# Rounding the running expert maximum to f16 on GpSimd instead of ScalarE, in a fused attention and max-out feed-forward kernel

## The chip, the cores and the metric

The kernel runs on one core of a Trainium2 chip. The metric is device time in microseconds; three runs of the kernel before gave 973.61, 969.4 and 974.53 us, a median of 973.61. Five engines of the core work side by side, each through its own queue in program order: TensorE (PE; its weight loads are shown apart as PEld), VectorE (DVE), ScalarE (ACT), GpSimd (POOL) and SyncE (SP), which issues most transfers. An instruction that waits holds up everything behind it in its own queue.

## The reference

Causal attention with a cumulative bias, for 8 batches of 8 heads, 576 positions and head size 64, and behind it a feed-forward layer that takes the largest of three projections:

```
scores = scale * q @ k.T + min(-(cum[q] - cum[k]), 0)     # causal; cum = cumsum(max(s, 0))
attn   = exp(scores - max) / (sum + 1e-9)
x      = (attn @ v), heads side by side                    # 4608 tokens x 512
h      = max(max(x @ w1, x @ w2), x @ w3)                  # 4608 x 768
out    = h @ w_out                                         # 4608 x 512
```

The products are kept near f32 by splitting an operand into an f16 part and the f16 remainder of it: a product is then three matmuls (high by high, high by low, low by high). For `h`, the high part is called `hh` and the remainder `hl = h - hh`.

## The kernel before

**Attention** is cut into visits (a batch and a pair of heads) and these into 160 steps, each a block of 128 query positions. One step t goes through the engines like this: TensorE makes the scores in a PSUM bank `s` (two banks, so the scores of step t+2 need the bank that step t leaves); VectorE takes the row maximum `nm` (L447, function `highest`); ScalarE takes the exponential and its sum (L457, L461, `expo`); VectorE the reciprocal `ri` (L480); ScalarE writes the probabilities rounded to f16, `prh` and for the last block `tl` (L496); VectorE writes their remainder `prl` (L499), after which the bank is free; SyncE transposes both by DMA, and TensorE multiplies them with the values (`av`, L552). ScalarE and VectorE evict that as `x` and its remainder (L562, L563).

**Feed-forward work** fills TensorE's time between the attention matmuls. When the 256 or 320 tokens of a set are complete (16 sets: 8 batches, each in two parts), `add_set` queues 18 `h_group`s (6 blocks of 128 hidden features, `ft`, by 3 experts, `i`), each of 12 matmuls into a PSUM tile `pm` (L679), and 4 `o_group`s of 18 matmuls into `po` (L721). An eviction follows each `h_group`: for expert 0 ScalarE copies `pm` to the SBUF tile `m` (L693); for experts 1 and 2 VectorE takes the larger of `pm` and `m` into `m` (L696). After expert 2 the function `rest` splits `m`: ScalarE writes `hh` (L685), and GpSimd `hl` (L686). The `o_group`s need `hh` and `hl` of all six blocks, in the order of the blocks; `o` is evicted by ScalarE (L729) with a scale `os` from GpSimd (L714).

**The order** is that in which the program is written out; nothing is reordered afterwards. In step t the main loop (L877) writes: the reciprocal and `prh` of t; `nm` of t+1; `prl` of t and its transposes; then `drain()`, the evictions that are pending, and `flush()`, every `rest` that they have left; perhaps one feed-forward group; the scores of t+2; the exponentials of t+1; `drain()` and `flush()` again; what prepares later steps (on ScalarE L150, L154, L346 and others, on VectorE L159, L351, on GpSimd L137 to L168); more groups, as long as a running cost estimate allows; and the `av` matmuls of a visit. So a `rest` of the first `flush()` stands on ScalarE ahead of the exponentials of the next step, and on GpSimd among the casts and subtractions that prepare the heads of later visits.

Of the kernel before, what the change touches and what calls it, by code (L numbers as in the profile page):

```python
# [14 lines left out]
AF = mybir.ActivationFunctionType  # L15
# [6 lines left out]
def kernel(  # L22
# [9 lines left out]
    nc = tc.nc  # L32
# [149 lines left out]
    def load_w(i, dma=None):  # L182
# [14 lines left out]
        out=tri, in_=tri, pattern=[[-1, P]], compare_op=ALU.is_ge, fill=NEG, base=0, channel_multiplier=1  # L197
    )
    nc.gpsimd.memset(tri4, 0.0)
    for j in range(2):  # L200
        r = slice(j * D, (j + 1) * D)
        nc.gpsimd.affine_select(
            out=tri4[r], in_=tri4[r], pattern=[[-1, D]], compare_op=ALU.is_ge, fill=NEG, base=0, channel_multiplier=1
# [457 lines left out]
    def drain():  # L661
        while pending:
            pending.pop(0)()

    def add_set(b, ph):
        q0, nq = PH[ph]
        t0 = b * S + q0
        u = f"{b}_{ph}"
        xs = [(t[:, i, 0], t[:, i, 1]) for t in X.pop((b, ph)) for i in range(2)]
        st = {}  # L670

        def h_group(ft, i):
            pm = ps_m.tile([P, 512], F32, tag="m", name=f"pm{u}_{ft}_{i}")
            w = W[3 * ft + i]
            n = 0
            for kt in range(NKT):
                xh, xl = xs[kt]
                for wt, xt in ((0, xh), (0, xl), (1, xh)):
                    nc.tensor.matmul(  # L679
                        pm[:, :nq], lhsT=w[:, wt, kt, :], rhs=xt, start=(n == 0), stop=(n == 3 * NKT - 1)  # L680
                    )
                    n += 1

            def rest(m1):
                nc.scalar.activation(out=st["hh"][:, ft, :nq], in_=m1[:, :nq], func=AF.Copy)  # L685
                nc.gpsimd.tensor_tensor(  # L686
                    out=st["hl"][:, ft, :nq], in0=m1[:, :nq], in1=st["hh"][:, ft, :nq], op=ALU.subtract
                )

            def ev():  # L690
                if i == 0:
                    st["m1"] = moe.tile([P, 320], F32, tag="m1", name=f"m1{u}_{ft}", bufs=3)
                    nc.scalar.activation(out=st["m1"][:, :nq], in_=pm[:, :nq], func=AF.Copy, scale=HSC)  # L693
                else:
                    m1 = st["m1"]
                    nc.vector.scalar_tensor_tensor(  # L696
                        out=m1[:, :nq], in0=pm[:, :nq], scalar=HSC, in1=m1[:, :nq], op0=ALU.mult, op1=ALU.max
                    )
                if i == 2:
                    if not st.get("hh"):  # L700
                        st["hh"] = moe.tile([P, NFT, 320], F16, tag="hh", name=f"hh{u}")
                        st["hl"] = moe.tile([P, NFT, 320], F16, tag="hlo", name=f"hl{u}")
                    later.append(lambda m1=st["m1"]: rest(m1))

            pending.append(ev)
            if (ft, i) == (NFT - 1, 2):
                done.add((b, ph))

        def o_group(dt):
            drain()  # L710
            flush()
            if dt == 0:
                st["os"] = small.tile([P, 1], F32, tag="os", name=f"os{u}")
                nc.gpsimd.tensor_scalar(  # L714
                    out=st["os"], in0=OS[b, ph if b < NB else 1], scalar1=WS["kw"], scalar2=None, op0=ALU.mult
                )
            pm = ps_m.tile([P, 512], F32, tag="m", name=f"po{u}_{dt}")
            n = 0
            for ft in range(NFT):
                for wt, ht in ((0, "hh"), (0, "hl"), (1, "hh")):  # L720
                    nc.tensor.matmul(  # L721
                        pm[:, :nq], lhsT=W[18 + ft][:, wt, dt, :], rhs=st[ht][:, ft, :nq],
                        start=(n == 0), stop=(n == 3 * NFT - 1),
                    )
                    n += 1

            def ev():
                o_t = moe.tile([P, 320], F32, tag="m1", name=f"o{u}_{dt}", bufs=3)
                nc.scalar.activation(out=o_t[:, :nq], in_=pm[:, :nq], func=AF.Copy, scale=st["os"])  # L729
                nc.sync.dma_start(out=outT[dt * P:(dt + 1) * P, t0:t0 + nq], in_=o_t[:, :nq])  # L730

            pending.append(ev)

        for ft in range(NFT):
            for i in range(3):
                queue.append((lambda ft=ft, i=i: h_group(ft, i), (3 * ft + i,), 12 * nq * NSEC))
        for dt in range(NDT):
            queue.append((lambda dt=dt: o_group(dt), range(18, 24), 18 * nq * NSEC))
# [3 lines left out]
    def flush():  # L742
        while later:
            later.pop(0)()
# [224 lines left out]
```

## Time and profile before

| | before |
|---|---|
| median of three runs | 973.61 us (969.4 to 974.53) |
| the profiled execution: span from its first to its last instruction | 972.4 us; the profile gives no other total for it |
| PE / ACT / DVE / POOL busy | 847.3 / 599.1 / 589.2 / 285.2 us |
| `hh` on ScalarE (L685) | 96 times, 42.3 us busy; ScalarE idle in front of them 105.3 us |
| `hl` on GpSimd (L686) | 96 times, 73.9 us busy; GpSimd idle in front of them 459.8 us |

A profile line names the line of the kernel, the engine, the operation and its tiles (written <- read, shapes as partitions x elements), then times. In a timeline the first number is the start and the second the duration in us, and a bracket gives the engine's idle time in front of the instruction and what ended it. "x2" merges two instructions of one kind. An arrow "A <- B" in a list of waits reads: A waited for B. A PE matmul's end is modelled, so its busy time contains the pipeline's length; back to back, matmuls overlap.

### The profile page before, as it was taken

What the parts mean: (1) busy time and instruction counts of PE and PEld (TensorE: products, weight loads), DVE (VectorE), ACT (ScalarE), POOL (GpSimd) and SP (SyncE); (2) the same over time, 40 slices, a digit from 0 to 9 for tenths busy, and PEclk for the clock granted to TensorE, in tenths of its full rate; (3) what the DMA queues carried; (4) which work ended last, traced back from release to release, by engine and by line L of the source; (5) the groups of instructions that cost most, each with busy time, mean ns of one, the idle gap of its engine ahead of it and who ended that gap; (6) DMA issues with size and microseconds to landing.
All of it is one profiled execution on the core that took longest, in us unless ns stands there. A gap on an engine that the chain in (4) does not pass through costs nothing. (4 is left out here: it accounts for less than half of the span.)

```text
span 972.4 us, 19924 instructions
## 1 busy us (share of the span) xinstructions
PE 847.3 (87%) x7192; PEld 658.6 (68%) x7192; DVE 589.2 (61%) x1216; ACT 599.1 (62%) x1598; POOL 285.2 (29%) x455
## 2 busy tenths in 40 slices
PE   2547759997889967999999998999999999999998
PEld 2435547775557746876788777877787778777876
DVE  6898876656546665656666566665666666554111
ACT  4657566565547676676667676666676676765121
POOL 2001221212333432333333433444343433320101
PEclk9756979999889978999999999999999999999999
DMA  8952245477467777676868676875867776734000
GB/s 299 261 149 61 82 89 128 109 134 141 93 134 145 132 159 134 126 151 117 155 115 151 120 159 111 151 140 121 150 114 143 130 156 115 140 66 97 5 24 28
DMA packets 242035, 122.34 MB, mean 126 GB/s; under 512 B 217808, under 2 KB 226512, under 8 KB 241936
## 3 DMA queue, kind: packets, MB, share of 16 engines
q1 hardware_dynamic: 237904, 108.74, 56.8%
q10 hardware_dynamic: 4032, 12.32, 4.1%
q8 instruction: 57, 0.93, 0.4%
q14 instruction: 42, 0.34, 0.2%
HBM read 60.18 MB, written 9.44 MB: 72 GB/s over the span
## 5 line engine op out<-in xcount | busy, mean ns | idle before, releaser
L679 PE MATMUL pm<-x,w 128*128 128x256 f16 (+1 forms) x3456 | 461.0, 290 | 10.9 <-DVE x L563 5.6
L679 PEld LDWEIGHTS <-w 128*128 128x128 f16 x3456 | 335.0, 99 | 99.3 <-issue 11.5
L499 DVE SCALAR_TENSOR_TENSOR prl<-s,ri,prh 128x512 f16<-128x512 f32 (+3 forms) x288 | 153.0, 568 | 109.4 <-ACT prh L496 75.5
L686 POOL TENSOR_TENSOR hl<-m,hh 128x256 f16<-128x256 f32 (+1 forms) x96 | 73.9, 770 | 459.8 <-ACT hh L685 429.8
L496 ACT ACTIVATE prh<-s,ri 128x512 f16<-128x512 f32 (+3 forms) x288 | 141.6, 538 | 41.5 <-DVE ri L480 31.3
L457 ACT ACTIVATE s<-s,nm 128x512 f32<-128x512 f32 (+4 forms) x288 | 150.9, 524 | 9.7 <-DVE nm L447 5.5
L721 PE MATMUL po<-hh,w 128*128 128x256 f16 (+1 forms) x768 | 153.0, 290 | 3.1 <-ACT hh L685 3.0
L696 DVE SCALAR_TENSOR_TENSOR m<-pm,m 128x256 f32<-128x256 f32 (+1 forms) x192 | 87.2, 454 | 106.3 <-PE pm L679 91.7
L447 DVE TENSOR_REDUCE nm<-s 128x1 f32<-128x576 f32 (+4 forms) x160 | 127.7, 798 | 37.0 <-PE s L382 24.4
L721 PEld LDWEIGHTS <-w 128*128 128x128 f16 x1152 | 111.9, 99 | 33.7 <-issue 5.5
L721 PE MATMUL po<-hl,w 128*128 128x320 f16 (+1 forms) x384 | 111.2, 290 | 1.6 <-POOL hl L686 1.6
L685 ACT ACTIVATE hh<-m 128x256 f16<-128x256 f32 (+1 forms) x96 | 42.3, 440 | 105.3 <-DVE m L696 105.3
L562 ACT ACTIVATE x<-av 128x256 f16<-128x256 f32 (+1 forms) x64 | 26.3, 411 | 78.4 <-PE av L552 78.3
L693 ACT ACTIVATE m<-pm 128x256 f32<-128x256 f32 (+1 forms) x96 | 38.9, 405 | 52.6 <-PE pm L679 52.4
L168 POOL TENSOR_TENSOR l<-raw,h 64x576 fp32r<-64x576 f32 x48 | 67.9, 1414 | 2.3 <-ACT h L154 0.7
L376 PE MATMUL s<-h 128*128 128x128 f32 (+1 forms) x192 | 54.9, 368 | 15.1 <-DVE prl L499 11.8
L563 DVE SCALAR_TENSOR_TENSOR x<-av,x 128x256 f16<-128x256 f32 (+1 forms) x64 | 29.1, 454 | 64.1 <-ACT x L562 64.1
L137 POOL CAST l<-kb 64x576 fp32r<-64x576 f32 x48 | 31.9, 666 | 113.0 <-PE s L391 100.7
L552 PEld LDWEIGHTS <-vh 128*64 128x64 f16 x832 | 45.0, 114 | 22.3 <-issue 13.4
L552 PE MATMUL av<-ph,vh 128*64 128x320 f16 (+3 forms) x384 | 57.9, 293 | 2.3 <-DMA ph<-prh 2.3
L729 ACT ACTIVATE o<-po,os 128x256 f32<-128x256 f32 (+1 forms) x64 | 31.9, 498 | 45.1 <-PE po L721 28.6
L552 PE MATMUL av<-pl,vh 128*64 128x320 f16 (+3 forms) x384 | 57.1, 285 | 2.8 <-DMA pl<-prl 2.5
(138 smaller groups left out, 1108.8 us busy)
## 6 DMA issues: line engine op xcount, KB each, us to landing
raw<-in_qk_dram SPq DMA_DIRECT2D x96, 304.0 KB, 4.8
r<-in_w_dram ACTq DMA_DIRECT2D x20, 512.0 KB, 4.8
rv<-in_qkv_dram SPq DMA_DIRECT2D x32, 320.0 KB, 3.3
out_dram<-o SPq DMA_DIRECT2D x32, 160.0 KB, 2.2
out_dram<-o SPq DMA_DIRECT2D x32, 128.0 KB, 2.2
raw<-in_qkv_dram SPq DMA_DIRECT2D x8, 480.0 KB, 3.8
ph<-prh SPq DMA_TRANSPOSE x192, 3.3
pl<-prl SPq DMA_TRANSPOSE x192, 2.8
```

What stands on the lines that cost most here:

```text
L168: nc.gpsimd.tensor_tensor(out=l[far, QP:V0], in0=raw[far, QP:V0], in1=h[far, QP:V0].bitcast(F32), op=ALU.subtract)
L376: nc.tensor.matmul(ps[:, j, :nk], lhsT=w[:, qs], rhs=w[:, QP:QP + nk], start=(x == "h"), stop=False, skip_group_check=True,)
L447: nc.vector.tensor_reduce(out=nm, in_=sc, axis=AX.X, op=ALU.max, negate=True)
L457: nc.scalar.activation(out=sc, in_=sc, func=AF.Exp, bias=nm[:, j:j + 1], accum_out=sm[:, j:j + 1])
L496: nc.scalar.activation(out=hi, in_=src, func=AF.Copy, scale=sc)
L499: nc.vector.scalar_tensor_tensor(out=lo, in0=src, scalar=sc, in1=hi, op0=ALU.mult, op1=ALU.subtract)
L552: nc.tensor.matmul(av[j * D:(j + 1) * D, c0:nq], lhsT=lt, rhs=rt, start=(n < 2), stop=(n >= len(todo) - 2), skip_group_check=True,)
L679: nc.tensor.matmul(pm[:, :nq], lhsT=w[:, wt, kt, :], rhs=xt, start=(n == 0), stop=(n == 3 * NKT - 1))
L685: nc.scalar.activation(out=st["hh"][:, ft, :nq], in_=m1[:, :nq], func=AF.Copy)
L686: nc.gpsimd.tensor_tensor(out=st["hl"][:, ft, :nq], in0=m1[:, :nq], in1=st["hh"][:, ft, :nq], op=ALU.subtract)
L696: nc.vector.scalar_tensor_tensor(out=m1[:, :nq], in0=pm[:, :nq], scalar=HSC, in1=m1[:, :nq], op0=ALU.mult, op1=ALU.max)
L721: nc.tensor.matmul(pm[:, :nq], lhsT=W[18 + ft][:, wt, dt, :], rhs=st[ht][:, ft, :nq], start=(n == 0), stop=(n == 3 * NFT - 1),)
```

## The change

One line of `rest` changes: the f16 copy `hh` of the running maximum is made by GpSimd, directly in front of the subtraction that reads it.

```diff
             def rest(m1):
-                nc.scalar.activation(out=st["hh"][:, ft, :nq], in_=m1[:, :nq], func=AF.Copy)
+                nc.gpsimd.tensor_copy(out=st["hh"][:, ft, :nq], in_=m1[:, :nq])
                 nc.gpsimd.tensor_tensor(
                     out=st["hl"][:, ft, :nq], in0=m1[:, :nq], in1=st["hh"][:, ft, :nq], op=ALU.subtract
                 )
```

On ScalarE, at the second block (`m_1_1`) of one set in the long middle of the program: `prh` and `tl` are the probabilities of a step, `hh` the rounding, `s` and `se` the exponentials and sum of the next step.

```order
 L496 ACTIVATE prh_7202<-s_7071,ri_7200 128x512
 L496 ACTIVATE tl_7204<-s_7071,ri_7200 128x64
-L685 ACTIVATE hh_1_7135<-m_1_1_7166 128x320
 L457 ACTIVATE s_7154,sm_7240<-s_7154,nm_7155 128x128 x2
 L461 ACTIVATE se_7243<-sm_7240 128x2
```

The exponentials of the next step now follow the probabilities directly. Two blocks later in the same set, again on ScalarE:

```order
 L457 ACTIVATE s_7277,sm_7398<-s_7277,nm_7278 128x384 x2
 L461 ACTIVATE se_7401<-sm_7398 128x2
 L154 ACTIVATE h_1_7297<-raw_1_7168 128x576
 L496 ACTIVATE prh_7425<-s_7277,ri_7423 128x3x128 x2
-L685 ACTIVATE hh_1_7135<-m_1_3_7371 128x320
 L457 ACTIVATE s_7390,sm_7461<-s_7390,nm_7391 128x512 x2
 L461 ACTIVATE se_7464<-sm_7461 128x2
```

Here too the probabilities and the next exponentials become neighbours. The same stretch of the set on GpSimd, where `h` and `l` are the two parts of a head's queries and keys for a later visit:

```order
 L142 MEMSET l_1_7298 64x64
 L143 CAST l_1_7298<-qr_362 64x64
+L685 CAST hh_1_7135<-m_1_2_7245 128x320
 L686 TENSOR_TENSOR hl_1_7136<-m_1_2_7245,hh_1_7135 128x320
 L163 CAST l_1_7298<-h_1_7297 64x640
+L685 CAST hh_1_7135<-m_1_3_7371 128x320
 L686 TENSOR_TENSOR hl_1_7136<-m_1_3_7371,hh_1_7135 128x320
 L137 CAST l_0_7470<-kb_359 64x576
```

Each cast stands directly in front of its subtraction. The orders on TensorE and VectorE are the same as before.

## The prediction

> **What bounds the kernel now.** I read the page's busy times first, then the engines by stage, then who waits for whom in the long middle stage, and last the timeline around TensorE's waits. First the page's busy line, and the engines in the two stages that hold the change (busy time and instruction count of each engine, granted TensorE clock, DMA share, GB/s):
>
> ```profile
> PE 847.3 (87%) x7192; PEld 658.6 (68%) x7192; DVE 589.2 (61%) x1216; ACT 599.1 (62%) x1598; POOL 285.2 (29%) x455
> ...
> 92.00:391.00 299.00, 247.75 (x2042) 187.71 (x2040) 189.10 (x372) 187.39 (x482) 83.31 (x119) 0.91 0.60 122
> 391.00:893.00 502.00, 481.51 (x4241) 378.61 (x4239) 312.07 (x641) 341.99 (x932) 181.68 (x286) 1.00 0.70 131
> ```
>
> The rounding starts at 92 us, and after 893 attention is over, which leaves these two. From 391 to 893 us TensorE is busy 481.5 of 502 us at full clock: nothing there can be worth more than 20.5 us. From 92 to 391 us it idles 51 us, and the clock averages 0.91.
>
> So an average ("ACT 62%") tells nothing; the question is what ends TensorE's 20.5 idle us in the middle, and whether the rounding stands in that chain. Waits, 391 to 893 us (waiter, releaser: us in total, times, longest):
>
> ```profile
> PE s L376 <- DVE prl L499: 9.1, 14, 1.0
> PE s L391 <- DVE prl L499: 5.1, 5, 1.0
> PE pm L679 <- DVE x L563: 4.7, 4, 1.2
> ...
> ACT hh L685 <- DVE m L696: 50.5, 40, 2.2
> ```
>
> TensorE mostly waits for the score bank that VectorE's prl (L499) frees. And ScalarE stands still 50.5 us in front of the very instruction that is moved, with the next step's exponentials queued behind it. The L391 wait comes 5 times, so the stage has five like repeats of some 100 us. In each stands such a place, called A:
>
> ```profile
> 534.44 5.05 PE L679 MATMUL pm<-x,w 128*128 128x320 f16 x36
> ...
> 535.28 0.41 DVE L447 TENSOR_REDUCE nm<-s 128x2 f32<-128x256 f32 x1
> ...
> 536.53 0.32 ACT L496 ACTIVATE tl<-s,ri 128x64 f16<-128x64 f32 x1
> ...
> 537.74 1.08 DVE L696 SCALAR_TENSOR_TENSOR m<-pm,m 128x320 f32<-128x320 f32 x2
> 538.86 0.47 ACT L685 ACTIVATE hh<-m 128x320 f16<-128x320 f32 x1 [2.01 <-DVE m L696]
> ...
> 539.23 0.32 ACT L457 ACTIVATE s<-s,nm 128x128 f32<-128x128 f32 x1
> ...
> 540.31 0.42 ACT L693 ACTIVATE m<-pm 128x320 f32<-128x320 f32 x1
> 540.63 0.82 ACT L346 ACTIVATE vh<-rv,inv 128x640 f16<-128x640 f32 x1
> 541.35 0.62 ACT L496 ACTIVATE prh<-s,ri 128x128 f16<-128x128 f32 x2
> ...
> 542.75 0.59 PE L376 MATMUL s<-h 128*128 128x384 f32 x2 [1.04 <-DVE prl L499]
> ```
>
> Read from the bottom: TensorE idles 1.04 us, for a prl that waited for prh, which stood behind L346, L693 and the exponential, which stood behind the rounding, which waited 2.01 us for VectorE's maximum. The exponential's own input, nm, was ready at 535.69.
>
> **The change part by part.** *Removed from ScalarE*: 96 activations. *Added to GpSimd*: 96 casts. The activation, the subtraction behind it, and the nearest casts on GpSimd (count; busy us, mean ns; idle before):
>
> ```profile
> L685 ACT ACTIVATE hh<-m 128x256 f16<-128x256 f32 (+1 forms) x96 | 42.3, 440 | 105.3 <-DVE m L696 105.3
> ...
> L686 POOL TENSOR_TENSOR hl<-m,hh 128x320 f16<-128x320 f32 x48 | 40.3, 840 | 216.8 <-ACT hh L685 205.8 <-DMA raw<-in_qk_dram 7.4 <-PE s L382 3.6
> L138 POOL CAST l<-qr 64x512 fp32r<-64x512 f32 x48 | 29.5, 614 | 0.0
> L143 POOL CAST l<-qr 64x64 fp32r<-64x64 f32 x48 | 12.0, 251 | 0.0
> ```
>
> ScalarE loses 42.3 us of work. The two cast rows give (614 - 251)/448 = 0.81 ns an element over about 199 ns: 0.41 us for 256 columns, 0.46 for 320, on the mean what ScalarE took. Bounds: not under the 0.25 of the smallest cast, and not over the 0.84 of the two-input subtraction. I take 0.41 and 0.46, the same operation on the same engine, though no row has an f16 output; in all some 42 us more on GpSimd, which is busy 182 of 502 us in the middle.
>
> *The hand-over.* The subtraction now waits for its own engine. A dependent pair on GpSimd stands in the trace, and beside it the tightest place, where the output matmuls need the last hl:
>
> ```profile
> 126.46 0.21 POOL L631 TENSOR_SCALAR rtd<-rtd 128x1 f32<-128x1 f32 x1
> 126.76 0.27 POOL L635 TENSOR_SCALAR kw<-rtd,rtu 128x1 f32<-128x1 f32 x1
> ...
> 922.29 0.42 ACT L685 ACTIVATE hh<-m 128x256 f16<-128x256 f32 x1 [2.63 <-DVE m L696]
> 922.78 0.67 POOL L686 TENSOR_TENSOR hl<-m,hh 128x256 f16<-128x256 f32 x1 [3.26 <-ACT hh L685]
> ...
> 923.51 0.27 PE L721 MATMUL po<-hl,w 128*128 128x256 f16 x1
> ```
>
> 126.76 - 126.67 = 0.09 us, against 922.78 - 922.71 = 0.07 today. So hl keeps its time, to within 0.02 us; with the slow cast it would be 0.4 us late, and the slack here is 923.51 - 923.45 = 0.06. Over 16 token sets that is at most 16 x 0.4 = 6 us, a bound I keep; I take 0. No DMA moves, and what is queued on GpSimd behind a cast waited there behind the subtraction before.
>
> *The wait.* It moves with the cast: GpSimd now waits for VectorE's maximum, where it had waited for ScalarE. On ScalarE nothing replaces it at A: the exponential can start when tl ends, 536.85, and with what follows it takes 540.31 - 539.23 = 1.08, to 537.9. Then L693 must wait for the third of the 36 matmuls' three groups, at 539.49 by the trace; L346 (0.32 later) comes at 539.8, prh (another 0.72) at 540.55 in place of 541.35, so 0.8 us sooner; ri is free by then, as VectorE's maxima end at 538.82. The 1.04 us shrinks to 0.24. The two other repeating kinds, B and C:
>
> ```profile
> 554.81 0.47 ACT L685 ACTIVATE hh<-m 128x320 f16<-128x320 f32 x1 [1.61 <-DVE m L696]
> 555.19 0.64 ACT L457 ACTIVATE s<-s,nm 128x512 f32<-128x512 f32 x1
> ...
> 560.69 0.41 PE L376 MATMUL s<-h 128*128 128x128 f32 x2 [0.83 <-DVE prl L499]
> ...
> 600.61 0.41 ACT L685 ACTIVATE hh<-m 128x256 f16<-128x256 f32 x1
> 600.92 0.55 ACT L457 ACTIVATE s<-s,nm 128x384 f32<-128x384 f32 x1
> ```
>
> At B the exponential comes 1.61 + 0.38 = 1.99 us sooner and TensorE's 0.83 goes. At C, in front of L391, the rounding found no wait: only 600.92 - 600.61 = 0.31 is saved. The L563 waits (4.7 us) have no rounding in their chain and stay. Middle stage: of L376's 9.1 us all but 5 x 0.24 = 1.2, so 7.9 (I let the five smallest of the 14 waits go with the rest); of L391's, 5 x 0.31 = 1.6; together 9.5 us (1.9 a repeat), between 0 (another wait steps in) and 14.2 (all of both rows).
>
> *Before 391 us.* Most of the 51 idle us end with a VectorE that is itself busy, or with loads and transposes. Two places have the rounding in their chain (ahead of them the roundings of this stage, by the source line):
>
> ```profile
> L685 ACT ACTIVATE hh<-m x26: 401/418/471, 92.3 to 387.8; 128x256 f16<-128x256 f32 x14, 128x320 f16<-128x320 f32 x12
> ...
> 125.33 0.42 ACT L685 ACTIVATE hh<-m 128x256 f16<-128x256 f32 x1 [1.54 <-DVE m L696]
> ...
> 132.69 0.36 PE L436 MATMUL s<-qkh 128*128 128x256 f32 x1 [2.46 <-DVE prl L499]
> ...
> 188.76 0.36 PE L436 MATMUL s<-qkh 128*128 128x256 f32 x1 [0.90 <-DVE prl L499]
> ```
>
> The first can give 1.54 + 0.32 = 1.9, the second its 0.9: 2.8 us. Against it stands a price on VectorE:
>
> ```profile
> L143 POOL CAST l<-qr x48: 227/238/879, 247.0 to 852.0; 64x64 fp32r<-64x64 f32 x48
> ...
> 339.37 0.87 DVE L351 SCALAR_TENSOR_TENSOR vl<-rv,inv,vh 128x640 f16<-128x640 f32 x1
> ...
> 568.39 1.41 POOL L168 TENSOR_TENSOR l<-raw,h 64x576 fp32r<-64x576 f32 x1
> ...
> 569.16 1.32 DVE L351 SCALAR_TENSOR_TENSOR vl<-rv,inv,vh 128x640 f16<-128x640 f32 x1
> ```
>
> A GpSimd cast of 238 ns took 879, the one at 339.47 beside a VectorE instruction with two SBUF inputs; the same VectorE instruction took 1.32 in place of 0.87 beside a GpSimd subtraction: 0.45 us a meeting. The Trainium skill (GPSIMD Engine Reference, 1. Specifications) states that GpSimd's SBUF interfaces are shared with VectorE, which conflicts when VectorE reads two SBUF inputs; by that rule the trace agrees, and the rule speaks against more GpSimd work. I take four such meetings on VectorE's path before 391 us, 1.8 us, so the early stage gives 2.8 - 1.8 = 1.0 us.
>
> **Sum.** 9.5 + 1.0 = 10.5 us off the profiled execution's span of 972.4: 961.9. The median of the runs shown, 973.6, lies 1.2 above that span; kept, this makes 963.
>
> **Rivals.**
> *Another wait steps in.* Freed of the rounding, ScalarE runs into L693's wait for TensorE, or VectorE is the late one. For it: at A that wait already keeps 0.24 us. Against it: at A and B the chain from exponential to prl has no idle time of ScalarE left. Then only C's 1.6 us go: 972.
> *GpSimd and VectorE collide (slower).* Casts follow VectorE's maximum at once, just when VectorE starts two-input work. 26 of the 96 roundings lie before 391 us; if all met it on VectorE's path, 26 x 0.45 = 12 us are lost, and with the middle gaining nothing the time is 973.6 + 12 = 986; it decides once 10.5/0.45, some 23, such meetings are on the path. For it: the 879 ns row. Against it: VectorE is idle 299 - 189 = 110 us of the early stage, and GpSimd did its subtraction beside the same work before.
> *The clock comes back (larger gain).* At 0.91 over 299 us TensorE loses 0.09 x 299 = 27 us, in stretches around its idle times. If shorter waits spare half of that, the time is 963 - 13 = 950. For it: the full clock in the dense middle. Against it: most early waits stay. The Trainium skill (TensorE: Matmul & The Clock Gate, Part 1) has the clock halved after an idle window and restored by a busy one; by that rule the trace agrees, at 1.00 where TensorE is dense.
> That the change is not what it says is out: the instruction order shows each pair moved as written.
>
> **How the numbers follow.** Forecast 0.56 (957 to 969), another wait 0.20 (969 to 974), collision 0.10 (975 to 986), clock 0.14 (945 to 957). What this kernel's measurement can tell is about 0.5%, 4.9 us. Faster than 968.7: nearly all of the forecast, 0.52, all of the clock case, 0.14, a little of the second, 0.02: 0.68. Slower than 978.5: most of the collisions, 0.08; I put 0.09. The rest, 0.23, is no change. The range 952 to 975 leaves out half of the clock case and the worse collisions, about 0.17.
>
> **What would show it.** Right: L685 appears on GpSimd at 0.41 and 0.46 us; the row "ACT hh L685 <- DVE m L696" is gone and the same wait stands before GpSimd's cast; TensorE's L376 waits for prl in the middle fall from 9.1 to near 1, L391's from 5.1 to about 3.5; each repeat shortens by some 2 us. Wrong: those waits stay with a different last link (L693 or ri), new waits of po for hl appear, or VectorE's L351, L159 and L652 get clearly longer.

## The result and the profile after

The changed kernel takes 959.69 us (median of 4 runs, 958.87 to 960.19). The kernel before, run beside it, takes 972.3 us (4 runs, 969.4 to 974.53). The ratio is 0.9876, with a 95% interval of 0.9856 to 0.9896: 1.24% or 12.6 us faster. The forecast was 963, in a range of 952 to 975, with 0.68 on "faster". The profiled execution of the changed kernel took 958.87 us, with a span of 957.1.

The page of the changed kernel, its busy line and the group of the moved instruction:

```profile
PE 843.1 (88%) x7192; PEld 657.5 (69%) x7192; DVE 586.0 (61%) x1216; ACT 567.7 (59%) x1502; POOL 339.1 (35%) x551
...
L685 POOL CAST hh<-m 128x256 f16<-128x256 f32 (+1 forms) x96 | 52.1, 542 | 384.0 <-DVE m L696 330.3
```

ScalarE has 96 instructions fewer and is busy 31 us less (its instructions overlap by some 0.1 us each, so the rounding's 42.3 us were not all time of its own); GpSimd has 96 more and is busy 54 us more. The wait for VectorE's maximum has moved with the rounding: 105 us in front of L685 on ScalarE before, 330 us in front of L685 on GpSimd now. On GpSimd it costs little: it had stood still there before as well, 459.8 us in front of the subtraction, and it is 35% busy.

Here is how the two stages look now (changed kernel; busy time of PE, PEld, DVE, ACT and POOL, then granted TensorE clock, DMA share, GB/s):

```profile
92.00:391.00 299.00, 250.30 (x2099) 190.97 (x2100) 189.20 (x378) 180.18 (x462) 98.46 (x148) 0.92 0.61 124
391.00:893.00 502.00, 487.67 (x4299) 385.91 (x4299) 311.51 (x642) 325.75 (x876) 217.68 (x345) 1.00 0.70 131
```

TensorE's idle time between 391 and 893 us has gone from 20.5 to 14.3 us. The two windows do not hold the same work, though: the changed kernel is ahead, and more of its quieter end lies inside. So the repeats have to be counted. These are the starts of the matmuls behind the wait at C, one repeat apart, in the kernel before:

```profile
503.17 0.48 PE L391 MATMUL s<-h 128*128 128x256 f32 x2 [1.02 <-DVE prl L499]
...
606.34 0.47 PE L391 MATMUL s<-h 128*128 128x256 f32 x2 [1.02 <-DVE prl L499]
```

And in the changed kernel:

```profile
495.99 0.47 PE L391 MATMUL s<-h 128*128 128x256 f32 x2 [0.71 <-DVE prl L499]
...
596.85 0.47 PE L391 MATMUL s<-h 128*128 128x256 f32 x2 [0.71 <-DVE prl L499]
```

A repeat takes 100.86 us in place of 103.17 between these rows, and of 103.1 on the mean of the four in that trace: 2.2 us less. At C the wait fell from 1.02 to 0.71. The waits of TensorE in the changed kernel, from 391 to 880 us, where the repeats end (us in total, times, longest):

```profile
PE pm L679 <- DVE x L563: 5.8, 5, 1.2
PE s L391 <- DVE prl L499: 3.6, 5, 0.7
PE s L376 <- DVE prl L499: 2.3, 9, 0.3
```

L376's waits fell from 9.1 to 2.3 us, L391's from 5.1 to 3.6. The L563 waits stayed, as no rounding stands in their chain (there are five of them now, since the last, earlier in this kernel, falls into the window).

Place A in the timeline of the changed kernel (start, duration; idle time and releaser in brackets):

```profile
528.41 0.32 ACT L496 ACTIVATE tl<-s,ri 128x64 f16<-128x64 f32 x1
528.61 0.35 ACT L457 ACTIVATE s<-s,nm 128x128 f32<-128x128 f32 x1
...
530.72 0.49 DVE L696 SCALAR_TENSOR_TENSOR m<-pm,m 128x320 f32<-128x320 f32 x1 [0.62 <-PE pm L679]
531.34 0.45 POOL L685 CAST hh<-m 128x320 f16<-128x320 f32 x1 [2.21 <-DVE ri L480]
531.87 0.79 POOL L686 TENSOR_TENSOR hl<-m,hh 128x320 f16<-128x320 f32 x1
...
532.35 0.44 ACT L693 ACTIVATE m<-pm 128x320 f32<-128x320 f32 x1 [2.55 <-PE pm L679]
532.68 0.82 ACT L346 ACTIVATE vh<-rv,inv 128x640 f16<-128x640 f32 x1
533.40 0.62 ACT L496 ACTIVATE prh<-s,ri 128x128 f16<-128x128 f32 x2
...
534.05 0.61 DVE L499 SCALAR_TENSOR_TENSOR prl<-s,ri,prh 128x128 f16<-128x128 f32 x2 [0.41 <-ACT prh L496]
...
534.81 0.59 PE L376 MATMUL s<-h 128*128 128x384 f32 x2 [0.27 <-DVE prl L499]
```

The exponential now starts 0.20 us after the start of `tl`. What ScalarE waits for next is L693, 2.55 us, for a group of matmuls that simply isn't done earlier. From there L346, prh, prl and the matmul follow as before, and TensorE's 1.04 us are 0.27. The cast takes 0.45 us, and the subtraction starts 0.08 us after it.

### The profile page after: what moved, and what is told of

The parts are those of the page before. It is cut to its first block, busy times and chain, and to the rows that moved or that the text cites. A ratio compares the mean times of both kernels' runs of the same rounds, so it can differ in the third digit from the quotient of the medians.

```text
span 957.1 us, 19956 instructions
## 1 busy us (share of the span) xinstructions
PE 843.1 (88%) x7192; PEld 657.5 (69%) x7192; DVE 586.0 (61%) x1216; ACT 567.7 (59%) x1502; POOL 339.1 (35%) x551
## 5 line engine op out<-in xcount | busy, mean ns | idle before, releaser
L499 DVE SCALAR_TENSOR_TENSOR prl<-s,ri,prh 128x512 f16<-128x512 f32 (+3 forms) x288 | 153.1, 568 | 89.3 <-ACT prh L496 56.7
L685 POOL CAST hh<-m 128x256 f16<-128x256 f32 (+1 forms) x96 | 52.1, 542 | 384.0 <-DVE m L696 330.3
L696 DVE SCALAR_TENSOR_TENSOR m<-pm,m 128x256 f32<-128x256 f32 (+1 forms) x192 | 87.3, 454 | 114.8 <-PE pm L679 95.2
L693 ACT ACTIVATE m<-pm 128x256 f32<-128x256 f32 (+1 forms) x96 | 39.1, 407 | 102.8 <-PE pm L679 102.7
L168 POOL TENSOR_TENSOR l<-raw,h 64x576 fp32r<-64x576 f32 x48 | 70.5, 1468 | 4.4 <-ACT h L154 2.8
L563 DVE SCALAR_TENSOR_TENSOR x<-av,x 128x256 f16<-128x256 f32 (+1 forms) x64 | 29.1, 454 | 62.6 <-ACT x L562 62.6
L376 PE MATMUL s<-h 128*128 128x128 f32 (+1 forms) x192 | 55.1, 369 | 8.1 <-DVE prl L499 4.4
```

The lines of the kernel that those rows point to most:

```text
L168: nc.gpsimd.tensor_tensor(out=l[far, QP:V0], in0=raw[far, QP:V0], in1=h[far, QP:V0].bitcast(F32), op=ALU.subtract)
L376: nc.tensor.matmul(ps[:, j, :nk], lhsT=w[:, qs], rhs=w[:, QP:QP + nk], start=(x == "h"), stop=False, skip_group_check=True,)
L499: nc.vector.scalar_tensor_tensor(out=lo, in0=src, scalar=sc, in1=hi, op0=ALU.mult, op1=ALU.subtract)
L685: nc.gpsimd.tensor_copy(out=st["hh"][:, ft, :nq], in_=m1[:, :nq])
L696: nc.vector.scalar_tensor_tensor(out=m1[:, :nq], in0=pm[:, :nq], scalar=HSC, in1=m1[:, :nq], op0=ALU.mult, op1=ALU.max)
```

## Experiments

The changed kernel was taken along twice more, as a yardstick on the same chips. The first time it ran beside three kernels that take the change apart into its two halves: the work that leaves ScalarE and the wait that leaves ScalarE.

### The changed kernel again

> The changed kernel again, as the measure for the three kernels beside it. All theories: 0.987 of the kernel before, some 12 us faster; the middle stage shows TensorE waiting for prl in front of L376 about 2.3 us and in front of L391 about 3.6 us.

Measured: 959.07 us, ratio 0.9873 (0.9844 to 0.9902). Later, beside the last kernel below, it took 957.99 us, ratio 0.9856 (0.9837 to 0.9875).

### Only the wait: a one-element copy stays on ScalarE

```diff
             def rest(m1):
+                dm = small.tile([P, 1], F32, tag="dm", name=f"dm{u}_{ft}")
+                nc.scalar.activation(out=dm, in_=m1[:, nq - 1:nq], func=AF.Copy)
                 nc.gpsimd.tensor_copy(out=st["hh"][:, ft, :nq], in_=m1[:, :nq])
```

> The changed kernel, with a 128x1 copy on ScalarE of the finished maximum put back where the rounding stood: the wait for VectorE returns to ScalarE's queue, with some 0.2 us of work in place of 0.44. Theory W (the wait in front of the exponentials is what cost): at A and B nearly all comes back, TensorE's L376 waits in the middle rise from 2.3 to about 8 us, L391's from 3.6 to about 4.5, and the time is 1 to 4 us below the kernel before. Rival L (ScalarE's 42 us of work are what cost): half of the work is still gone, so about half of the gain stays, 6 us below before, and L376's waits lie near 5 us. Rival G (the gain is that hl comes sooner on GpSimd): nothing is lost, 12 us below before.

Measured: 963.48 us, ratio 0.991 (0.9881 to 0.9938). Some 8 us of the gain are there although the wait was put back whole, some 6 of them in the repeats (five times 1.2 us, see below). The waits of this kernel, 391 to 880 us, TensorE's and ScalarE's:

```profile
PE s L376 <- DVE prl L499: 5.2, 13, 0.6
...
PE s L391 <- DVE prl L499: 4.0, 5, 0.8
...
ACT dm L685 <- DVE m L696: 51.4, 40, 2.2
```

ScalarE stands as long as before (51.4 us, against 50.5), and TensorE waits only 5.2 us for L376's bank in place of 9.1. The theory that the wait makes the gain expected at most 4 us here; the rival that ScalarE's work makes it, with 6 us and L376 near 5, came nearer. The mistake of the first is seen at place A of this kernel:

```profile
528.86 0.20 ACT L685 ACTIVATE dm<-m 128x1 f32<-128x1 f32 x1 [0.90 <-DVE m L696]
...
529.63 5.05 PE L679 MATMUL pm<-x,w 128*128 128x320 f16 x36
...
531.38 0.31 ACT L496 ACTIVATE tl<-s,ri 128x64 f16<-128x64 f32 x1
...
532.59 1.08 DVE L696 SCALAR_TENSOR_TENSOR m<-pm,m 128x320 f32<-128x320 f32 x2
533.70 0.20 ACT L685 ACTIVATE dm<-m 128x1 f32<-128x1 f32 x1 [2.01 <-DVE m L696]
533.81 0.32 ACT L457 ACTIVATE s<-s,nm 128x128 f32<-128x128 f32 x1
...
537.33 0.58 PE L376 MATMUL s<-h 128*128 128x384 f32 x2 [0.42 <-DVE prl L499]
```

ScalarE's wait is 2.01 us, as it was. But it ends earlier: VectorE's maximum is done at 533.67, 4.04 us after the 36 matmuls begin, where the kernel before needs 538.82 - 534.44 = 4.38. Part of the maximum's lateness is ScalarE's own doing. The maximum is queued on VectorE behind prl and tl (L499), these wait for ScalarE's prh and tl, these for the exponentials, and these stand behind the *previous* rounding. So a part of the wait is a link of a closed chain: rounding, exponential, probabilities, VectorE's remainder, VectorE's maximum, next rounding. It is the smaller part: in the changed kernel, where no rounding stands in the chain, the second maximum waits for TensorE instead (530.72, 0.62 us) and ends 3.95 us after the matmuls begin. At most 4.38 - 3.95 = 0.43 of the 2.01 us come from the chain; for the rest the matmuls are not done. At A the maximum comes 0.34 us sooner here, and the rounding behind it holds the exponential for 0.11 us (533.81 - 533.70) where it held it for 0.37 (539.23 - 538.86), 0.26 less. Together these are 0.60, and TensorE's wait at A fell by 0.62, from 1.04 to 0.42.

### Only the work: ScalarE copies a constant of the same size

In front of the cast, ScalarE copies a constant tile into the place of `hl`, which GpSimd then overwrites. ScalarE has all the work of the rounding again (41.6 us, against 42.3) and no wait for the maximum.

```diff
             def rest(m1):
+                nc.scalar.activation(out=st["hl"][:, ft, :nq], in_=KB[0][:, :nq].bitcast(F32), func=AF.Copy)
                 nc.gpsimd.tensor_copy(out=st["hh"][:, ft, :nq], in_=m1[:, :nq])
```

> The changed kernel, with a copy of the rounding's size on ScalarE in the rounding's place, of a constant tile into hl's place (which the subtraction then overwrites): the work returns without the wait for the maximum. Theory W: A and B stay as in the changed kernel (L376's waits 2.3 to 3 us), only C's 0.31 us a repeat comes back (L391's waits 3.6 to about 5 us), and the time is 9 to 11 us below before. Rival L: the whole gain goes, 0 to 2 us below before. Rival G: a loss of 1 us at most, since hl now waits for ScalarE as well.

Measured: 959.97 us, ratio 0.9875 (0.9846 to 0.9903). All but about one us of the gain is there with ScalarE's work put back. TensorE's waits, 391 to 880 us:

```profile
PE s L391 <- DVE prl L499: 5.1, 5, 1.0
...
PE s L376 <- DVE prl L499: 2.3, 9, 0.3
```

This separates the two kinds of place. L376's waits are those of the changed kernel: there the wait decided, as the theory of the wait said, and a theory of ScalarE's load alone falls. L391's are those of the kernel before: at C, where the rounding had found no wait, its 0.31 us of work were all there was to gain.

### The rounding stays on ScalarE, behind the next exponentials

```diff
         next(parts)
         drain()
-        flush()
         if ready() and cost[0] > 0:
             run_group()
```

> The kernel before, rounding on ScalarE, with the first flush of a step taken out, so that a rounding stands behind the next step's exponentials: the work stays on ScalarE, and by then the maximum is there. Theory W: B's waits go, A keeps some 0.3 more than in the changed kernel (the rounding still stands ahead of L346 and prh), C is as before: L376's waits 3 to 5 us, L391's 5 us, 4 to 8 us below before. Rival L: as before, 0 to 1 us. Rival G: hl comes later than before, so as before or slower.

Measured: 964.21 us, ratio 0.9923 (0.9894 to 0.9952), some 7 us faster. The waits, 391 to 880 us:

```profile
PE s L391 <- DVE prl L499: 5.1, 5, 1.0
...
PE s L376 <- DVE prl L499: 4.1, 9, 0.6
...
ACT hh L685 <- DVE m L696: 26.6, 25, 2.2
```

No instruction changes engine here; only the places of the rounding and of its subtraction in their queues change. That alone brings more than half of the gain, as the theory of the wait expected (4 to 8 us). ScalarE's wait halves.

A repeat takes 103.1 us before. It is shorter by 1.2 us with most of the work gone and the wait kept, by 1.9 with the wait gone and the work kept, by 1.4 with the rounding moved behind, and by 2.2 us with both gone (101.9, 101.2, 101.7 and 100.9 us). The first two don't add up to the last, 3.1 against 2.2, and they need not: both shorten the same chain, until L693 limits it.

### GpSimd for the first four sets only, and for the other twelve only

Set out against the kernel before; `nset` numbers the sets from 0, and the lines that count it are left out:

```diff
-                nc.scalar.activation(out=st["hh"][:, ft, :nq], in_=m1[:, :nq], func=AF.Copy)
+                if nset < 4:        # the second kernel: nset >= 4
+                    nc.gpsimd.tensor_copy(out=st["hh"][:, ft, :nq], in_=m1[:, :nq])
+                else:
+                    nc.scalar.activation(out=st["hh"][:, ft, :nq], in_=m1[:, :nq], func=AF.Copy)
```

> The rounding on GpSimd for the first 4 of the 16 token sets only (24 of the 96 roundings, up to about 335 us), on ScalarE as before for the rest. By the prediction's terms (2.8 us of waits less 1.8 us of collisions): 1 us below the kernel before, with the middle's waits as before (L376 9.1, L391 5.1 us). By the first profile of the changed kernel, which came to 391 us of the middle some 5 us sooner: 3 to 5 us below. By the collision rival: above the kernel before.

> The other part alone: the rounding on GpSimd for sets 5 to 16, on ScalarE for the first 4. By the theory that ScalarE's chain of the middle stage is what was shortened: L376's waits 2.3 us, L391's 3.6, a repeat of about 100.9 us in place of 103.1, and 9.5 to 11 us below the kernel before. With early_sets it should add up to the whole change, some 12 us, if the two parts are independent.

Measured: the first four sets alone give 969.63 us, ratio 0.9975 (0.9957 to 0.9992), so 0.25%, or 2.4 us (0.8 to 4.2). The twelve later ones alone give 962.29 us, 0.9888 (0.9867 to 0.9909), so 1.12%, or 10.9 us. Together 1.37%, against 1.24 to 1.44% for the whole change in its three comparisons: the two parts add up within the intervals. The early stage of the two (first four sets, then the later ones):

```profile
92.00:391.00 299.00, 250.70 (x2109) 191.75 (x2108) 191.55 (x382) 181.54 (x468) 97.59 (x145) 0.93 0.62 125
```

```profile
92.00:391.00 299.00, 247.92 (x2073) 188.92 (x2071) 190.98 (x376) 186.71 (x481) 83.81 (x121) 0.91 0.61 122
```

With the early sets changed, TensorE is 250.7 us busy in this stretch (250.3 with the whole change); without, 247.9 (247.75 before): 2.5 to 3 us more of its work gets done. The profiles of all the kernels here agree in the direction: 249.5 to 252.5 us in the eight with the early casts on GpSimd, 247.6 to 248.2 in the four without. The kernels with the wait or the work put back on ScalarE are among the eight (250.6 and 251.0), and the one with the rounding on VectorE, below, is among the four. So the early gain does not follow ScalarE's relief alone.

### The rounding on VectorE

```diff
-                nc.scalar.activation(out=st["hh"][:, ft, :nq], in_=m1[:, :nq], func=AF.Copy)
+                nc.vector.tensor_copy(out=st["hh"][:, ft, :nq], in_=m1[:, :nq])
```

> The rounding on VectorE, directly behind its own maximum: ScalarE's and GpSimd's queues are as relieved as they can be, VectorE gets 96 copies of some 0.3 us (estimated from its 0.42 us for 512 columns in one instruction at 99.65 us). By the theory of ScalarE's chain: the middle as in the changed kernel within 1 us a stage, but before 391 us VectorE itself ends most waits, and 26 copies of 0.3 us cost up to 8 us there: 4 to 9 us below the kernel before, 3 to 8 above the changed one. If GpSimd's collisions cost the changed kernel much, this one is the faster.

Measured: 965.41 us, ratio 0.9917 (0.9891 to 0.9943): faster than before and, as expected, slower than the changed kernel, by some 4 to 6 us. The larger of its two groups on VectorE, and the early stage:

```profile
L685 DVE CAST hh<-m 128x320 f16<-128x320 f32 x48 | 15.6, 324 | 1.4
```

```profile
92.00:391.00 299.00, 248.24 (x2042) 188.93 (x2042) 195.72 (x398) 177.44 (x456) 85.32 (x116) 0.90 0.61 121
```

VectorE does the copy faster (324 ns for 320 columns) than either other engine, and it needs no wait, as it stands behind the maximum anyway. Still it isn't the best place. Before 391 us VectorE has 195.7 us of work in place of 189.1, and TensorE's 248.2 busy us there are nearly those of before: the early stage gains nothing. A repeat takes 101.1 to 101.3 us, 0.3 to 0.4 more than in the changed kernel.

### Every cast twice on GpSimd

```diff
                 nc.gpsimd.tensor_copy(out=st["hh"][:, ft, :nq], in_=m1[:, :nq])
+                nc.gpsimd.tensor_copy(out=st["hh"][:, ft, :nq], in_=m1[:, :nq])
```

> The changed kernel with every cast made twice, so hl comes one cast later and GpSimd collides with VectorE up to twice as often. By the prediction (hl has slack in the middle, little at the two ends of the last sets and at two early places; collisions cost little): 1 to 3 us above the changed kernel. By the collision rival (0.45 us a meeting on VectorE's path): 8 us or more above. If po waits for hl in the middle stage too, that shows as new waits of L721 there, up to 0.5 us for each of 10 sets.

Measured: 963.95 us, ratio 0.9908 (0.9888 to 0.9928), so 3 to 5 us above the changed kernel by its ratios, a little more than the 1 to 3 expected and well below the 8 of the collision theory. TensorE's waits for the two halves of the hidden features, in the whole of this kernel:

```profile
PE po L721 <- POOL hh L685: 4.6, 2, 3.9
...
PE po L721 <- POOL hl L686: 2.3, 5, 0.6
```

And in the changed kernel:

```profile
PE po L721 <- POOL hh L685: 3.1, 1, 3.1
PE po L721 <- POOL hl L686: 1.6, 2, 1.0
```

So 2.2 us of it are a later `hl` and `hh` in front of the output matmuls, none of them in the repeats; the L376 and L391 waits of the repeats are those of the changed kernel, to the tenth. The rest, one to three us, I cannot place. VectorE's L351 takes 35.3 us in all, against 30.8 in the changed kernel, but the repeats are only some 0.07 us longer.

### The wait that is left: x in front of prl

The largest wait that the change leaves in the repeats is that of pm for x (L563, 1.23 us each). The kernel: where the output that completes a set is the only eviction pending, it is evicted ahead of prl.

The line that sets `full` up is left out:

```diff
-        pending.append(out)
+        pending.append(out); full[0] = g == NP - 1
...
         if t + 1 < len(steps):
             highest(t + 1)
+        full[0] = drain() if full[0] and len(pending) == 1 else None
         next(parts)
```

> The changed kernel, and where the attention output that completes a set is the only eviction pending, x (L562, L563) is evicted ahead of prl in place of behind it. It takes up the wait that the change leaves in the middle: pm<-x (L679) for VectorE's x (L563), 1.23 us a repeat. In the timeline of the changed kernel the output matmuls end at 573.3 us and ScalarE's x at 574.5, while VectorE works from 574.26 to 575.67 on prl and ends x at about 576.0. With x first, VectorE could end it at about 575.0. If that queue on VectorE is the cause, the L563 wait falls from 1.23 to about 0.2 a place and the time by 4 x 1.0, some 3 to 5 us, to 954 to 957. If the later prl (some 0.6 us) is then the late one, the wait reappears before L376 or L391 and the time stays within 1 us of the changed kernel.

> The changed kernel itself again, beside the next kernel: about 959 us, ratio 0.987 to the kernel before. From 391 to 880 us TensorE waits for VectorE's x (L563) 5.8 us, for L391's bank 3.6 and for L376's 2.3.

Measured: 963.99 us, ratio 0.9909 (0.9879 to 0.9939), against the 0.9856 (0.9837 to 0.9875) of the changed kernel beside it: not faster, but slower. TensorE's waits, 391 to 880 us, and one of the places:

```profile
PE s L376 <- DVE prl L499: 6.4, 13, 1.0
...
PE pm L679 <- DVE x L563: 0.8, 4, 0.2
```

```profile
578.49 0.42 DVE L563 SCALAR_TENSOR_TENSOR x<-av,x 128x256 f16<-128x256 f32 x1 [1.03 <-ACT x L562]
578.83 1.40 DVE L499 SCALAR_TENSOR_TENSOR prl<-s,ri,prh 128x512 f16<-128x512 f32 x2
...
578.96 0.38 PE L679 MATMUL pm<-x,w 128*128 128x256 f16 x2 [0.19 <-DVE x L563]
...
580.37 0.41 PE L376 MATMUL s<-h 128*128 128x128 f32 x2 [1.03 <-DVE prl L499]
```

The L563 wait fell to 0.19 us as meant, and 1.4 us later a wait of 1.03 for prl stands in front of L376: VectorE has both x and prl to do, and at this place whichever comes second is late. That is the second of the two expected ways. It predicted no change; the 5 to 6 us that the kernel lost are in part a repeat of some 101.1 in place of 100.86 us, and the remainder lies before the repeats and in a single longer one. I did not follow it further. The changed kernel is the fastest that was found.

## Why the prediction was right, point by point

**The place A, and its new limit: right.** The forecast was that the wait at A falls from 1.04 to 0.24 us, since ScalarE would then wait for L693's group of matmuls. It fell to 0.27, behind exactly that wait.

**B and C: right.** No L376 wait longer than 0.3 us is left in the repeats, so B's 0.83 are gone. C was to lose the 0.31 us that the rounding occupies ScalarE, and went from 1.02 to 0.71. That this is work and not wait is shown by the kernel with the work put back, where C is 1.02 again.

**L376 and L391 in sum: right.** Forecast: 9.1 to 1.2 and 5.1 to 3.5. Measured: 2.3 and 3.6. The difference at L376 is the small waits that I let go with the rest: nine waits are left, not five. Still each repeat shortened by 2.2 us rather than the 1.9 forecast. In the repeat shown, L376's waits fell from 2.1 to 0.5 us and L391's from 1.02 to 0.71, which is the 1.9. The other 0.4 stands in TensorE's busy time: 98.66 us before (503.17 to 606.34), 98.26 now (495.99 to 596.85), for the same matmuls. Since a matmul's end is modelled, TensorE's idle time was no strict bound of what the stage could gain.

**The reason, that the wait is what costs: right, but not the whole.** The prediction took the work and the wait as two terms: the work counted only where there was no wait. The one-element copy showed 8 us of gain with the wait still there, 6 of them in the repeats. The step that failed is in the reading of the bracket "[2.01 <-DVE m L696]": I took VectorE's maximum as a time given from outside, while up to 0.43 of the 2.01 us came from a piece of VectorE's queue that itself waited for ScalarE. The forecast for the change held since both terms vanish in it together. The forecast for the kernel with the wait alone put back did not hold; that for the kernel with the work put back did.

**The early stage: 1.0 us was too low by the traces, and its terms were wrong.** It was 2.8 us of gain less 1.8 for four collisions on VectorE's path, 1.0 in all. The first four sets alone gave 2.4 us by their ratio (0.8 to 4.2), which does not exclude 1.0; but 2.5 to 3 us more of TensorE's work fits into the stretch. The charge of 1.8 was wrong. VectorE's busy time there was 189.10 us before (372 instructions) and is 189.20 now (378), and over the whole kernel the instructions of the charge got shorter: L159 from a mean of 886 ns to 861, and L351 as these lines show. Before:

```profile
L351 DVE SCALAR_TENSOR_TENSOR vl<-rv,inv,vh 128x640 f16<-128x640 f32 x32 | 31.8, 993 | 0.0
```

And in the changed kernel:

```profile
L351 DVE SCALAR_TENSOR_TENSOR vl<-rv,inv,vh 128x640 f16<-128x640 f32 x32 | 30.8, 963 | 0.0
```

By place, the 2.8 was not right. Of the two waits that were to give it, the one before L436 at 130 us gave 0.75 and not 1.9, and that at 188 us stayed at 0.9, with the exponential's sum as its new last link. Another wait, before the gate's matmul L280 at 138 us, fell from 3.97 to 3.08, and that was a meeting of GpSimd and VectorE. L280 waits for VectorE, which has three L652 to do first. Before:

```profile
133.33 3.64 DVE L652 SCALAR_TENSOR_TENSOR w<-r,swd,w 128x512 f16<-128x512 f32 x3
...
134.57 1.85 POOL L324 TENSOR_TENSOR qkl<-raw,qkh 128x576 fp32r<-128x576 f32 x1
```

And in the changed kernel:

```profile
132.84 2.62 DVE L652 SCALAR_TENSOR_TENSOR w<-r,swd,w 128x512 f16<-128x512 f32 x3
...
134.87 1.84 POOL L324 TENSOR_TENSOR qkl<-raw,qkh 128x576 fp32r<-128x576 f32 x1
```

Before, the last L652 started behind GpSimd's L324 and took 1.89 us; now the cast keeps GpSimd busy longer, the last L652 starts ahead of L324 and takes 1.15. The wait before L280 is 3.1 us or less in all eight kernels with the early casts on GpSimd and 4.0 to 4.4 in the other four. So at this place the collisions, charged as a loss, gave 0.9 us. That the 2.8 agrees with what the stage gained is luck. The rest of the early gain was not traced to its places.

**The casts, 0.41 and 0.46 us: right alone, too low on the mean.** The page has 542 ns for the mean of the two shapes. Apart from the collisions they take 0.40 and 0.45 us, but 27 of the 96 stand beside VectorE instructions with two SBUF inputs, and 21 of these take 0.85 to 1.03. One of them:

```profile
552.36 0.81 DVE L159 SCALAR_TENSOR_TENSOR h<-raw,h 64x640 fp32r<-64x640 f32 x1
552.51 0.97 POOL L685 CAST hh<-m 128x320 f16<-128x320 f32 x1 [1.51 <-DVE m L696]
```

**The hand-over and hl: right.** The subtraction follows 0.08 us behind the cast (0.09 forecast). The wait of the output matmuls for hl is 1.6 us in two places, before and after.

**The rivals.** *Another wait steps in* was right at one point only, L693 at A, whose 0.24 us were in the forecast already. *GpSimd and VectorE collide* is refuted by the time and by the doubled cast: the meetings are there, but GpSimd pays for most of them in its idle time, and VectorE's rows are no longer than before. *The clock comes back* didn't happen: 0.91 before, 0.92 now, from 92 to 391 us.

**The sum.** Against the runs beside it the change gives 12.6 us where 10.5 were forecast. The interval of the ratio reaches from 10.1 to 14.0 us, so the times alone show no surplus. By the medians it lies in both stages: the later sets alone gave 10.9 us (8.9 to 12.9) where 9.5 were forecast for the middle, the early ones 2.4 where 1.0 was. The other 1.3 of the 3.3 us between 963 and 959.7 is the kernel before itself, at 972.3 in the four runs beside the change and 973.6 in the three shown.

## What to carry to other kernels

When an engine stands in front of an instruction with critical work queued behind it, ask two things: can that instruction go to a queue that has time to wait, and does what it waits for depend, around a few corners, on the same engine. As far as it does, the wait and the work are one chain, shortening either helps, and the two gains don't add. And what an instruction takes on an engine says little about where it belongs: the rounding is fastest on VectorE (0.32 us, against 0.45 on GpSimd), and there it was worth less; VectorE's queue is the one that TensorE's waits end at, which I take for the reason, though no run shows it by itself.

## What was not expected of the hardware

When GpSimd and VectorE met in these traces, the one that started second paid. In the changed kernel 27 of the 96 casts ran beside a VectorE instruction with two SBUF inputs (L159, L351 or L652). In 21 of them VectorE's had started 0.10 to 0.22 us earlier: it took no longer than alone (0.81 us for the L159 shown), and the cast took 0.85 to 1.03 us for work of 0.40 to 0.45. In the other six the cast started first and took 0.45 us, and the L159 beside it 0.94 to 1.01. The Trainium skill (GPSIMD Engine Reference, 1. Specifications) states that the two share their SBUF interfaces and conflict when VectorE reads two SBUF inputs; by that rule the trace agrees, in these casts.

The prediction had charged the meetings to VectorE, from one row where a GpSimd subtraction, which reads two inputs, stood beside L351. Its two rows already show the order: the cast of 879 ns started 0.10 us after its L351, and the L351 of 1.32 us started 0.77 us after its subtraction. A cast waits for VectorE's maximum, and VectorE starts its next instruction at once, so a cast mostly starts second. With each cast made twice, L351's mean rose from 963 to 1102 ns, so VectorE does not always go free:

```profile
L351 DVE SCALAR_TENSOR_TENSOR vl<-rv,inv,vh 128x640 f16<-128x640 f32 x32 | 35.3, 1102 | 0.0
```

Here too it goes by the start: the 9 that started ahead of GpSimd's instruction took 0.88 us, the 17 that started behind one 1.30 on the mean.
